# Column DFT by parity of rows in the second layer, sums of halves that accumulate, and another opening

## The chip, the cores and the metric

One core of one Trainium2 chip runs the whole kernel. The metric is the device time of one execution in microseconds (us). Five engines work side by side: TensorE (PE, matrix products; its weight loads are PEld), VectorE (DVE), ScalarE (ACT), GpSimd (POOL) and SyncE (SP), which issues transfers; DMA queues move data between HBM and the on-chip memory. PSUM is the memory of eight banks into which TensorE writes.

## The reference

Two layers, each an FNet step (Fourier mixing of a sequence of 2048 rows and 640 hidden columns) and a gated linear unit of width 1728:

```python
def _A_ref(x, dft_seq_re, dft_seq_im, dft_hid_re, dft_hid_im):
    a = jnp.einsum("bsd,ed->bse", x, dft_hid_re)
    b = jnp.einsum("bsd,ed->bse", x, dft_hid_im)
    return jnp.einsum("ts,bse->bte", dft_seq_re, a) - jnp.einsum("ts,bse->bte", dft_seq_im, b)

def _B_ref(x, w_gate, w_up, w_down):
    g = jnp.einsum("bsd,df->bsf", x, w_gate)
    u = jnp.einsum("bsd,df->bsf", x, w_up)
    return jnp.einsum("bsf,fd->bsd", _sigmoid(g) * u, w_down)

x = A_x
x = x + _A_ref(_layernorm(x), ...)      # layer 1
x = x + _B_ref(_layernorm(x), ...)
x = x + _A_ref(_layernorm(x), ...)      # layer 2
x = x + _B_ref(_layernorm(x), ...)
```

## The kernel before

All values are float32, and each product is made of f16 parts: a number is split into a high and a low part, and hi x hi, hi x lo and lo x hi are added in PSUM. The four DFT matrices have the symmetries of cosine and sine; the kernel uses them to fold x by columns and by rows, so that the products are of a quarter of the size. x stays on the chip, as 16 row tiles of 128.

**One FNet step.** `fold_columns` (L627, L628, DVE) adds and subtracts column d and column 640 - d; `fold_rows` (L667 to L673) and `fold_join` (L707 sums on DVE, L709 high parts on ACT, L715 low parts on DVE) do the same for row s and row 2048 - s. The reversed rows that this takes come from TensorE: `turn_round` (L355) multiplies by a reversed identity into the pair of banks `twin`, and `turned` (L361, ACT) takes them out. Layer norm is folded in: `stats` of each row (L420 on DVE, or ACT), `smeans` and `power` (L377, L403, L404 on GpSimd), `scale` (L408 to L413, L656 on DVE). The opening does this for four groups of rows, 0 to 3, taken from HBM; layer 2 does it block by block, as the layer before ends.

Then `sequence(i, tp)` (L846, L850, TensorE, 18 matmuls of 256 columns) multiplies by the matrix along the sequence: group i, even or odd (EV, OD) outputs. `evict_sums` (L241 on ACT, L243 on DVE) takes the sums out as high and low parts, z. `hidden(q, ph)` (L923, TensorE) multiplies half ph of z by the hidden matrix, for row block q: 9 matmuls for its real part and 8 for its imaginary part, of 321 columns. There are four row blocks and two halves, so eight such products in a layer, and `hidden_middle` (9 matmuls with one row). `evict_hidden` (L959 on ACT, L964 on DVE), `combine` (L989), `join_hidden` (L996) and `add_hidden` (L1009) on DVE form the four outputs that the symmetries give, and add them to x. For q = 0 this is on the way to the next layer norm; the other row blocks follow later, beside products.

**One gated unit.** `norm_*` (L443 on DVE, L430 and L431 on ACT, L453, L463, L465) normalizes a row tile, `transpose_pe` (L569) turns it on TensorE, `gate_up` (L1134) makes the gates and `seven` (L1181, L1274, L1269) the products of later blocks with fewer multiplications, `down` (L1338) the second matrix, whose sums L1353 (DVE) adds to x. Four blocks of rows; these take most of TensorE's time.

**What sets the order.** Everything is placed by hand. The string `OPENING` lists the jobs of the opening and of layer 1's DFT in the order in which they are issued: "seq 3 0" is `sequence(3, EV)`, "hid 0 0" `hidden(0, 0)`, "jlo 3 e" the low part of the even fold of group 3, "evhi 0 1 2" and "ev 0 1 2" the eviction of sums. After it TensorE's work stands in the list `steps`, and `at(u, f, ...)` puts a job of the other engines beside step u. Each engine runs its own queue in order. `Slots` gives out the on-chip memory. The matrix parts for the hidden products (`load_wh`, `split_wh`, keys "h") are split in layer 1 and kept in HBM for layer 2.

Of the kernel before, what the change touches and what calls it, by code (L numbers as in the profile page):

```python
# [16 lines left out]
P = 128  # L17
# [13 lines left out]
EC = EH + 1  # L31
EPS = 1e-5
# [39 lines left out]
FIX = XU + 2 * XTU + WDU  # L72


class Slots:

    LOOK = {4: 2, 5: 6}

    def __init__(self, big):
        self.big = big
        self.live = {}
        self.freed = {}
        self.clock = 0
        self.close = False

    def take(self, n, high):
        taken = sorted(self.live.values())
        if self.close:  # L90

            ends = [FIX] + [d for _, d in taken]
            free = [(a, b) for a, b in zip(ends, [c for c, _ in taken] + [UNITS]) if a + n <= b]
            assert free, f"no room for {n}: {taken}"
            if high:
                a = [a for a in range(UNITS - n, FIX - 1, -n) if all(a + n <= c or d <= a for c, d in taken)][:high]
                if a:
                    return self.new(min(a, key=lambda a: max(self.freed.get(u, 0) for u in range(a, a + n))), n)
                a = max(b for _, b in free) - n
            else:  # L100
                a = min((a for f in free for a in {f[0], f[1] - n}),
                        key=lambda a: (max(self.freed.get(u, 0) for u in range(a, a + n)), a))
            return self.new(a, n)
        found = []
        for i in range(UNITS):
            a = UNITS - (i + 1) * n if high else FIX + i * n
            if a < FIX or a + n > UNITS:
                break
            if all(a + n <= c or d <= a for c, d in taken):
                found.append(a)  # L110
                if len(found) == self.LOOK.get(n, 3):
                    break
        if not found:
            found = [a for a in range(FIX, UNITS - n + 1) if all(a + n <= c or d <= a for c, d in taken)][:1]
        assert found, f"no room for {n}: {taken}"
        age = lambda a: max(self.freed.get(u, 0) for u in range(a, a + n))
        return self.new(min(found, key=age), n)

    def new(self, a, n):
        s = Slot(self.big[:, a * UNIT : (a + n) * UNIT], (a, a + n))  # L120
        self.live[id(s)] = s.span
        return s

    def give(self, s):
        self.clock += 1
        del self.live[id(s)]
        for u in range(*s.span):
            self.freed[u] = self.clock


class Slot:
    def __init__(self, ap, span):
        self.f32, self.span = ap, span
# [19 lines left out]
    turn 0 B, turned 0 B, turn 0 C, turned 0 C, turn 1 B, chi 0 0, means 0, chi 1 0, square 0 C, stats 0 A,  # L153
    col 0 0, stats 0 D, turned 1 B, turn 1 C, col 0 1, clo 0 0, square 0 B, turned 1 C, clo 1 0, double 0 0,
    smeans 0, double 0 1, stats 1 A, means 1, stats 1 D, col 1 0, col 1 1, chi 1 1, square 1 B, clo 1 1,
    square 1 C, power 0, turn 2 B, double 1 1, turned 2 B, turn 2 C, scale 0, stats 2 A, ro 0 0, chi 1 2, chi 0 1,
# [19 lines left out]
    wslo 3 0, wslo 4 0, wslo 4 1"""  # L176

ON_ACT = {(2, GA), (2, GD), (3, GA), (3, GD)}
NORM_ACT, APPLY_ACT, COPY_ACT = {0, 3}, {3}, {3}


@with_exitstack
# [1733 lines left out]
```

## Time and profile before

| | |
|---|---|
| median of 3 runs | 1143.39 us (1142.93 to 1144.43) |
| span of the profiled execution | 1142.6 us |
| TensorE busy | 1107.9 us |
| VectorE busy | 757.1 us |
| ScalarE busy | 521.8 us |
| GpSimd busy | 372.3 us |
| TensorE's idle time before the first long run of matmuls of 512 columns at 109.68 us | some 28 us |

Read it by stage: the opening (to about 66.7 us) folds x while TensorE waits; then TensorE works through layer 1's hidden products and the gated units without pauses; at 603.7 us the head of layer 2 begins (folds of the last row block, sequence and hidden products, the norm of the first rows), and its gated units run from 634 us to the end. Matmuls are pipelined, so the time of one is taken from an unbroken piece of the chain of waits divided by its count, not from the mean of a group.

### The profile page before, as it was taken

The numbers are of one execution on the slowest core, as the hardware profiler recorded it, in microseconds if no ns is written. First come the engines' busy times: TensorE is split into PE (matmuls) and PEld (weight loads), VectorE is DVE, ScalarE is ACT, GpSimd is POOL, SyncE is SP. The second block draws the span as 40 slices with busy tenths as digits, with TensorE's granted clock in tenths as the row PEclk, the third lists the DMA queues.
The fourth block names the chain that finished last, engine by engine and source line by source line (L and its number), as shares of the span: only waits on it lengthen the run. The fifth ranks groups of instructions, "written<-read, shape, count | busy, mean of one in ns | idle before, by whom it ended". The sixth has DMA issues, their size and how long they took to land.

```text
span 1142.6 us, 23152 instructions
## 1 busy us (share of the span) xinstructions
PE 1107.9 (97%) x8918; PEld 876.1 (77%) x8918; DVE 757.1 (66%) x1686; ACT 521.8 (46%) x1129; POOL 372.3 (33%) x584
## 2 busy tenths in 40 slices
PE   5599999999999999999999999999999999999997
PEld 2377446788878887888877888778887888788875
DVE  7995888867756777576657767815773568526740
ACT  5975475254524653265524445314551455225420
POOL 2313574432545454422430136021453113221000
PEclk9999999999999999999999999999999999999999
DMA  8427587858495868867412377575658853896401
GB/s 256 145 67 258 199 310 210 256 189 265 153 261 179 263 205 163 276 227 263 155 70 93 106 224 213 133 240 182 210 150 234 285 179 124 159 250 205 149 18 38
DMA packets 156434, 215.94 MB, mean 189 GB/s; under 512 B 74720, under 2 KB 101493, under 8 KB 156314
## 3 DMA queue, kind: packets, MB, share of 16 engines
q1 hardware_dynamic: 137754, 166.44, 48.1%
q0 software_dynamic: 18560, 47.93, 13.8%
q8 instruction: 72, 1.18, 0.4%
q14 instruction: 48, 0.39, 0.1%
HBM read 173.45 MB, written 26.26 MB: 175 GB/s over the span
## 4 chain that ended last, share of the span: by engine, by line
PE 89%; DVE 5%; DMA 2%; ACT 2%; issue 1%; POOL 1%; SPq 0%; DVEq 0%; POOLq 0%; ACTq 0%
PE acc L1181 42%; PE acc L1338 31%; PE acc L1134 10%; PE acc L1274 2%; PE acc L923 2%; PE acc L846 1%; DMA big<-in_ct 1%; DVE big L243 1%; PE twin L355 1%; DMA big<-kept_w 0%; DMA big<-in_wd 0%; DVE big L715 0%; DVE big L673 0%; DVE big L1009 0%; DVE big L707 0%
## 5 line engine op out<-in xcount | busy, mean ns | idle before, releaser
L1181 PE MATMUL acc<-big 128*128 128x256 f16 x4698 | 516.4, 273 | 0.2 <-ACT big L1185 0.2
L1181 PEld LDWEIGHTS <-big 128*128 128x128 f16 x4698 | 459.7, 98 | 54.6 <-issue 0.3
L1338 PE MATMUL acc<-big 128*128 128x320 f16 x2624 | 357.7, 299 | 0.0
L1338 PEld LDWEIGHTS <-big 128*128 128x128 f16 x2624 | 256.8, 98 | 99.5
L1387 POOL DMA_DIRECT2D big<-in_ct x256 | 174.8, 688 | 217.0 <-DVE big L1396 132.8
L1185 ACT ACTIVATE big<-acc 128x256 f32<-128x256 f32 x348 | 128.6, 380 | 237.0 <-PE acc L1181 235.6
L1371 ACT ACTIVATE big<-big 128x768 f32<-128x768 f32 (+8 forms) x104 | 79.6, 765 | 118.4 <-DVE big L1396 83.4
L1249 DVE TENSOR_TENSOR big<-big 128x512 f16<-128x512 f32 x87 | 59.9, 688 | 100.3 <-ACT big L1248 100.0
L1134 PE MATMUL acc<-big 128*128 128x256 f16 (+1 forms) x705 | 114.8, 325 | 1.1 <-DVE big L243 1.1
L1134 PEld LDWEIGHTS <-big 128*128 128x128 f16 x705 | 68.6, 98 | 46.2 <-DVE big L243 1.6
L1353 DVE SCALAR_TENSOR_TENSOR big<-acc,big 128x320 f32<-128x320 f32 x64 | 28.4, 484 | 99.4 <-PE acc L1338 99.3
L1227 ACT ACTIVATE big<-big 128x512 f32<-128x512 f32 x87 | 53.5, 627 | 45.2 <-DVE big L1218 44.6
L243 DVE SCALAR_TENSOR_TENSOR big<-big 128x640 f16<-128x640 f32 (+5 forms) x80 | 64.3, 839 | 9.9 <-ACT big L241 6.8
L241 ACT ACTIVATE big<-big 128x640 f16<-128x640 f32 (+6 forms) x80 | 50.2, 667 | 36.3 <-DMA big<-big 11.0
L1237 DVE SCALAR_TENSOR_TENSOR big<-acc,big 128x256 f32<-128x256 f32 x87 | 36.3, 418 | 40.5 <-PE acc L1181 34.4
L1404 POOL DMA_DIRECT2D big<-in_ct x40 | 27.3, 685 | 109.7 <-ACT big L1185 65.3
L1218 DVE TENSOR_TENSOR big<-big,acc 128x512 f32<-128x512 f32 x87 | 59.1, 679 | 3.6 <-PE acc L1181 3.4
L1248 ACT ACTIVATE big<-big 128x512 f16<-128x512 f32 x87 | 54.5, 626 | 9.6 <-DVE big L1239 8.8
L1217 DVE TENSOR_TENSOR big<-big 128x256 f32<-128x256 f32 x87 | 36.3, 417 | 15.6 <-ACT big L1185 15.5
L521 ACT ACTIVATE big<-big 128x384 f16<-128x384 f32 (+2 forms) x48 | 28.8, 648 | 29.3 <-DVE big L503 15.7
L1394 DVE TENSOR_TENSOR big<-big 128x256 f32<-128x256 f32 x64 | 26.8, 419 | 21.3 <-DMA big<-in_ct 21.2
L923 PE MATMUL acc<-big 128*128 128x321 f16 (+2 forms) x290 | 40.9, 300 | 0.0
(206 smaller groups left out, 1040.9 us busy)
## 6 DMA issues: line engine op xcount, KB each, us to landing
big<-kept_s SPq DMA_DIRECT2D x84, 512.0 KB
big<-kept_w SPq DMA_DIRECT2D x115, 320.0 KB
big<-in_ct POOLq DMA_DIRECT2D x256, 128.0 KB, 4.1
big<-kept_w SPq DMA_DIRECT2D x74, 192.0 KB
kept_w<-big SPq DMA_DIRECT2D x27, 320.0 KB
big<-in_ct POOLq DMA_DIRECT2D x32, 256.0 KB, 5.0
kept_s<-big SPq DMA_DIRECT2D x13, 512.0 KB
big<-in_wg SPq DMA_DIRECT2D x18, 320.0 KB
```

Of the source, the lines that this page charges most:

```text
L243: nc.vector.scalar_tensor_tensor(dl, src, s, dh, op0=OP.mult, op1=OP.subtract)
L923: nc.tensor.matmul(ps[:m, :EC], z[:, at : at + m], w[:, 384 * wp : 384 * wp + EC], start=(d == 0 and zp == HI and wp == HI), stop=(d == ND ...
L1134: nc.tensor.matmul(ps, w[wp][:, d * P : (d + 1) * P], xt[:, xp, :], start=(d == 0 and wp == HI and xp == HI), stop=(d == ND - 1 and wp == LO))
L1181: nc.tensor.matmul(ps, wt, xt, start=start and n == 0, stop=n == len(todo) - 1, skip_group_check=not start)
L1185: nc.scalar.activation(dst, ps, AF.Copy)
L1218: nc.vector.tensor_tensor(v, v, other, op=OP.add)
L1227: nc.scalar.activation(v, v, AF.Sigmoid, scale=SG)
L1248: nc.scalar.activation(s.parts[HI], v, AF.Copy)
L1249: nc.vector.tensor_tensor(s.parts[LO], v, s.parts[HI], op=OP.subtract)
L1338: nc.tensor.matmul(held["pd", e][0][:, :EH], held["ht", j].parts[hp][:, i * P : (i + 1) * P], held["w", 2, j].parts[wp][:, e * EH : (e + 1 ...
L1371: nc.scalar.activation(v, v, AF.Square, accum_out=new_sum()[:p])
L1387: nc.gpsimd.dma_start(v[:, g], bass.AP(ct.tensor, (r * S + row) * S, [[P, NS], [d * S, 16], [1, P]]))
```

## The change

1. In layer 2 the hidden products use one more symmetry: hidden index d and 320 - d. Rows of the hidden matrix are loaded by parity (`load_wh` with a stride of two rows, `fold_columns` writes even and odd columns apart), and only 161 of the 321 output columns are multiplied, for even and for odd rows into halves E and O of a bank. `unfold` makes the 321 columns again as E + O and E - O. Layer 1 stays at 321 columns (`wide`). For it the matrix is read from HBM and split a second time, instead of being kept.
2. Where halves ph = 0 and 1 of a row block were taken out of PSUM one by one and added by DVE, the second accumulates in PSUM onto the first, after ACT has copied the first: in layer 1 for all row blocks, in layer 2 for q = 0. The difference is then 2u - v.
3. In the opening the means, the edge copies and the first row's sum go from GpSimd to ScalarE, the variances to VectorE, and the power -0.5 to ScalarE's `Abs_reciprocal_sqrt` with one step of refinement on VectorE (`root`, `root_step`). `twin` becomes two pairs of banks, with four banks of sums in place of six until the turning is done.
4. `OPENING` is in another order, and so is the head of layer 2; the last `down` product of layer 1 is split by column halves, with the folds of its rows in halves. The sums and additions of row blocks 2 and 3 come earlier in the first block.
5. `Slots` takes its places from a planner that knows all uses beforehand (`find_homes`).

The core of the diff:

```diff
-    jhi 3 o, ev 0 0 1, join 3 e, jhi 3 e, jlo 3 o, seq 2 0, wshi 1 0, jlo 3 e, hid 0 0, wslo 1 0, seq 3 0, difhi 0,
+    seq 2 1, jhi 3 o, join 3 e, wshi 1 1, jhi 3 e, wshi 1 0, jlo 3 o, seq 2 0, jlo 3 e, ev 0 0 2, ev 0 0 1, whlo 2,
+    seq 3 0, evhi 1 0 2, evhi 1 0 1, evhi 1 0 0, wslo 1 1, hid 0 0, seq 3 1, first 0, ev 1 0 2, ev 1 0 0, ev 1 0 1,
...
+    twins = [twin_pool.tile([P, 2, 512], F32, name=f"twin{k}") for k in range(2)]
...
     def turned_means(i):
-        nc.gpsimd.tensor_scalar(t[:, GB:GD, 12], t[:, GB:GD, 20], 1.0 / D, None, op0=OP.mult)
+        nc.scalar.activation(t[:, GB:GD, 12], t[:, GB:GD, 20], AF.Copy, scale=1.0 / D)
...
+    def root(t, to):
+        nc.scalar.activation(t[:, :, 15], t[:, :, 14], AF.Abs_reciprocal_sqrt, scale=1.0 / to**2)
...
-    def product(ps, ph, r, at, m):
-        for d, n in enumerate(KT[r]):
+    def product(ps, ph, r, at, m, more=False):
+        even, odd, both = (slice(0, EC),) * 3 if wide else (slice(0, EW), slice(EW, EQ), slice(0, EQ))
+        for d, c in ((1, both), (0, even), (2, odd)):
+            n = KT[r][d]
...
-                    nc.tensor.matmul(ps[:m, :EC], z[:, at : at + m], w[:, 384 * wp : 384 * wp + EC],
-                                     start=(d == 0 and zp == HI and wp == HI), stop=(d == ND // 2 and zp == LO))
+                    nc.tensor.matmul(ps[:m, c], z[:, at : at + m], w[:, 384 * wp : 384 * wp + c.stop - c.start],
+                                     start=(not more and d == 1 and zp == HI and wp == HI),
+                                     stop=(d == ND // 2 and zp == LO), skip_group_check=more)
...
+    def unfold(s, v, on=nc.vector):
+        on.tensor_tensor(s[:, :, :EW], v[:, :, :EW], v[:, :, EW:], op=OP.add)
+        on.tensor_tensor(s[:, ::-1, EH : EW - 1 : -1], v[:, :, : EW - 1], v[:, :, EW : EQ - 1], op=OP.subtract)
...
-            order = [(hidden, 0, 0), (hidden, 1, 0), (sequence, 2, EV), (sequence, 2, OD), (sequence, 3, EV),
-                     (sequence, 3, OD), (hidden, 0, 1), (hidden, 2, 0), (hidden, 3, 0), (hidden, 1, 1), (hidden, 2, 1),
-                     (hidden, 3, 1), (hidden_middle,)]
+            order = [(hidden, 1, 0), (sequence, 0, OD), (sequence, 1, OD), (sequence, 2, EV), (sequence, 3, EV),
+                     (hidden, 0, 0), (hidden, 0, 1), (sequence, 2, OD), (sequence, 3, OD), (hidden, 1, 1), (hidden, 2, 0),
+                     (hidden, 3, 0), (hidden_middle,), (hidden, 2, 1)]
...
-            run(he + 12, [(transpose_pe, 0), (transpose_pe, 1)])
+            run(he + 12, [(evict_hidden, 3, 0), (transpose_pe, 0), (transpose_pe, 1), odd[5][1]])
```

TensorE's queue in layer 2 before, at the joint of the real part of hid 0 0 (into bank 67) and its imaginary part (bank 64):

```order
8838 L923 LDWEIGHTS big
8839 L923 MATMUL acc_67<-big 128x321
8840 L923 LDWEIGHTS big
8841 L923 MATMUL acc_64<-big 128x321
8842 L923 LDWEIGHTS big
8843 L923 MATMUL acc_64<-big 128x321
```

The same queue after, inside the real part of hid 1 0, which now comes first; L1031 is the line that was L923:

```order
8761 L1031 LDWEIGHTS big
8762 L1031 MATMUL acc_64<-big 128x322
8763 L1031 LDWEIGHTS big
8764 L1031 MATMUL acc_64<-big 128x161
8765 L1031 LDWEIGHTS big
8766 L1031 MATMUL acc_64<-big 128x161
```

Three matmuls of a part stay at 322 columns (both halves E and O), the rest have 161; their number and their weight loads stay.

VectorE's queue in the head of layer 2 before, from the last evictions of sums (L243) to the first row's statistics; 964 takes hid 0 1 out of PSUM, 996 joins the halves, 1009 adds to x:

```order
884 L243 SCALAR_TENSOR_TENSOR big<-acc_66,big 128x512
885 L243 SCALAR_TENSOR_TENSOR big<-acc_67,big 128x512
886 L243 SCALAR_TENSOR_TENSOR big<-acc_64,big 128x512
887 L964 SCALAR_TENSOR_TENSOR big<-acc_69,big 128x321 x2
888 L996 TENSOR_TENSOR big<-big 128x642
889 L1009 TENSOR_TENSOR big<-big 128x2x321
890 L1009 TENSOR_TENSOR big<-big 128x2x319
891 L443 BN_STATS small_81<-big 128x6 x2
```

The same place after; 267 evicts sums, 1099 takes the accumulated product, 1072 and 1073 unfold, 1181 adds to x:

```order
889 L267 SCALAR_TENSOR_TENSOR big<-acc_366,big 128x512
890 L267 SCALAR_TENSOR_TENSOR big<-acc_66,big 128x512
891 L267 SCALAR_TENSOR_TENSOR big<-acc_67,big 128x512
892 L1099 SCALAR_TENSOR_TENSOR big<-acc_64,big 128x322 x2
893 L1072 TENSOR_TENSOR big<-big 128x2x161
894 L1073 TENSOR_TENSOR big<-big 128x2x160
895 L1181 TENSOR_TENSOR big<-big 128x2x321
896 L1181 TENSOR_TENSOR big<-big 128x2x319
897 L488 BN_STATS small_79<-big 128x6 x2
898 L489 BN_AGGR small_79<-small_79 128x2
```

The join of halves has gone from this place and two unfolding operations have come in; the odd sums, which were all evicted ahead of it, are in part evicted after it.

VectorE's queue at the last fold of the opening before: 145 is "jlo 3 e", the low part of group 3's even fold, and 141 an eviction of sums:

```order
140 L673 SCALAR_TENSOR_TENSOR big<-big,quad_79 128x321
141 L243 SCALAR_TENSOR_TENSOR big<-acc_68,big 128x512
142 L707 TENSOR_TENSOR big<-big 128x321 x2
143 L715 TENSOR_TENSOR big<-big 128x2x320
144 L718 COPY big<-big 128x4x64
145 L715 TENSOR_TENSOR big<-big 128x2x321
146 L243 SCALAR_TENSOR_TENSOR big<-big 128x640 x2
```

After, the same fold stands at 148, and two evictions of sums follow it directly:

```order
143 L769 SCALAR_TENSOR_TENSOR big<-big,quad_77 128x321
144 L267 SCALAR_TENSOR_TENSOR big<-acc_363,big 128x512
145 L806 TENSOR_TENSOR big<-big 128x321 x2
146 L814 TENSOR_TENSOR big<-big 128x2x320
147 L817 COPY big<-big 128x4x64
148 L814 TENSOR_TENSOR big<-big 128x2x321
149 L267 SCALAR_TENSOR_TENSOR big<-acc_364,big 128x512
150 L267 SCALAR_TENSOR_TENSOR big<-acc_67,big 128x512
```

Before that fold VectorE evicts sums six times in the order before, four times after.

More of the change, by code (lines that the diff above doesn't have):

```diff
@@ L72, with __init__ @@
 FIX = XU + 2 * XTU + WDU
+NEAR = (60, 25, 8, 1)
 class Slots:
[L79 to L84, printed above, removed]
+    def __init__(self, big, homes=None):
+        self.big, self.homes = big, homes
+        self.asked = []
         self.clock = 0
-        self.close = False
     def take(self, n, high):
[L89 to L117, printed above, removed]
@@ L152 @@
 OPENING = """
[L153 to L156, printed above, removed]
-    smeans 1, turned 2 C, whhi 1, col 2 0, double 1 0, power 1, re 0 0, clo 1 2, ro 0 1, scale 1, whhi 2, ro 1 1,
```

502 lines of the change are left out of this document (346 added, 156 removed).

## The prediction

> **What bounds the kernel now.** I read the page's busy times and slices first, then the windows by stage, the timelines of TensorE (PE) and VectorE (DVE) where a window shows idle time, and last the chain of waits.
>
> ```profile
> span 1142.6 us, 23152 instructions
> PE 1107.9 (97%) x8918; PEld 876.1 (77%) x8918; DVE 757.1 (66%) x1686; ACT 521.8 (46%) x1129; POOL 372.3 (33%) x584
> PE   5599999999999999999999999999999999999997
> ```
>
> TensorE is busy for 1107.9 of 1142.6 us; 34.7 us are idle, by the slices almost all in the first two and at the very end. Elsewhere only fewer matmul columns save time. Five windows show the two stages that the change touches (columns after the length: PE, PEld, DVE, ACT, POOL busy, then the clock):
>
> ```profile
> 20.00:40.00 20.00, 7.55 (x14) 3.73 (x14) 17.20 (x48) 17.55 (x40) 8.21 (x10) 1.00 0.88 292
> 40.00:57.00 17.00, 11.67 (x75) 8.72 (x74) 16.31 (x41) 15.29 (x33) 4.22 (x14) 0.90 0.13 42
> 57.00:66.63 9.63, 9.19 (x75) 6.95 (x72) 9.56 (x20) 6.94 (x15) 0.21 (x1) 0.99 0.38 98
> 66.69:108.60 41.91, 41.84 (x367) 33.89 (x367) 28.56 (x54) 25.77 (x48) 12.66 (x16) 1.00 0.50 162
> 603.70:634.20 30.50, 29.80 (x240) 21.95 (x238) 25.28 (x57) 16.44 (x34) 3.44 (x6) 1.00 0.28 98
> ```
>
> Up to 66.63 VectorE sets the pace (9.56 of the last 9.63 us): it folds x for the DFT, and the last fold releases the last sequence products. From there TensorE is full (41.84 of 41.91). The head of layer 2, in the last row, has TensorE busy for 29.80 of 30.50 us, but VectorE is at 25.28 there too, so both are near their limits.
>
> The joints of the opening, from the timelines (start, length, what, and the idle time before it in brackets):
>
> ```profile
> 7.50 2.50 PE L355 MATMUL twin<-big 128*128 128x320 f32 x4 [0.88 <-ACT big L361]
> 7.48 0.83 DVE L627 TENSOR_TENSOR big<-big 128x640 f32<-128x640 f32 x1 [1.48 <-ACT big L361]
> 10.87 0.82 DVE L627 TENSOR_TENSOR big<-big 128x640 f32<-128x640 f32 x1 [0.79 <-ACT big L361]
> 20.82 0.17 DVE L408 TENSOR_TENSOR quad<-quad 128x4 f32<-128x4 f32 x1 [0.53 <-POOL quad L404]
> 25.55 0.70 DVE L243 SCALAR_TENSOR_TENSOR big<-big 128x514 f16<-128x514 f32 x1 [1.65 <-ACT big L241]
> 26.46 0.17 DVE L408 TENSOR_TENSOR quad<-quad 128x4 f32<-128x4 f32 x1 [0.22 <-POOL quad L404]
> 66.69 3.89 PE L846 MATMUL acc<-big 128*128 128x256 f16 x34 [0.50 <-DVE big L715]
> 109.68 10.53 PE L1134 MATMUL acc<-big 128*128 128x512 f16 x48 [1.14 <-DVE big L243]
> ```
>
> **The narrower products of layer 2.** Prices of a matmul come from unbroken pieces of the chain (start, length, what, how many):
>
> ```profile
> 70.58 13.96 PE acc L923 x102
> 559.34 44.43 PE acc L1338 x327
> 640.88 1.24 PE acc L569 x20
> 1011.47 71.39 PE acc L1181 x654
> L569 PEld LDWEIGHTS <-big 128*128 128x128 f16 x80 | 4.9, 98 | 1.3 <-DVE big L465 0.9
> ```
>
> So 321 columns take 13.96/102 = 0.1369 us, 320 columns 0.1359, 256 columns 0.1092: 0.417 ns per column more. Down that line 161 columns take 0.0697 us, 322 columns 0.1367. The transposes, 128 columns, take 0.062 where the line gives 0.056, so the line may be 6 ns too low: 0.076 at most that way. The loads of weights last 98 ns each, but twenty followed one another in 1.24 us there, so they overlap one another.
>
> Before, a product of layer 2 is 9 + 8 = 17 matmuls of 321 columns, 2.327 us. After, it is 3 of 322 and 6 of 161, then 3 of 322 and 5 of 161: 6 x 0.1367 + 11 x 0.0697 = 1.587 us. That is 0.740 less, 5.92 for eight. The middle row's 9 matmuls lose 957 columns, 0.40 us. Together **-6.3 us**, with 0.076 instead -5.7 (94 matmuls of 161 x 6 ns back). If each narrow matmul instead waited for its own 98 ns load, 94 x 28 ns = 2.7 us would come back and -3.6 remain. I take -6.3, since the transposes are the nearest row.
>
> The Trainium skill, "TensorE: Matmul & The Clock Gate", section "Back-to-back issue gap", speaks against this: it gives about 81 ns per matmul for a stream of weight load and matmul at 128 columns. By that a 161-column matmul would cost at least 81 ns, and the saving would be 5.2 us as an estimate. The transposes, at 62 ns a matmul in such a stream, are below that figure here.
>
> **What VectorE pays for it.** The outputs now come as even and odd halves, and each row block needs two more operations to unfold them, of 322 and 320 elements:
>
> ```profile
> L707 DVE TENSOR_TENSOR big<-big 128x321 f32<-128x321 f32 x2 | 0.9, 486 | 0.0
> 634.00:662.00 28.00, 28.00 (x237) 22.11 (x236) 20.98 (x35) 11.04 (x18) 2.50 (x9) 1.00 0.51 138
> ```
>
> Sixteen at 0.486 are 7.8 us. Four lie in the head, the others in stretches where VectorE has 7 of 28 us free, under TensorE's products; those cost nothing. The column folds now read every second element. A split that also reads so took 0.69 us for 516 elements, and 0.69 for 512 read straight:
>
> ```profile
> 50.68 0.69 DVE L243 SCALAR_TENSOR_TENSOR big<-big 128x516 f16<-128x516 f32 x1
> 52.39 0.68 DVE L243 SCALAR_TENSOR_TENSOR big<-acc,big 128x512 f16<-128x512 f32 x1
> ```
>
> So striding is free.
>
> **The head of layer 2.** Two chains must stay hidden. Their pieces before:
>
> ```profile
> 603.79 0.89 DVE big L1353 x2
> 613.56 3.56 PE acc L846 x31
> 619.48 0.45 ACT big L959
> 624.20 0.93 ACT big L431 x2
> 625.74 0.73 POOL small L404
> 631.57 0.83 DVE big L465
> ```
>
> The first, from the last sums of the layer before to the folds, takes 613.56 - 603.79 = 9.8 us. The change splits the last down product and folds its half columns early, so some 2 us of it go ahead of TensorE's last matmul, and 1.6 of odd folds behind the even ones; what is left, about 7 us, has hid(1,0) and two sequence products in front of it (1.6 us and 36 x 0.1092 = 3.9 us, beside the last half of the down product). The second chain, from the last product of block 0 to the turned rows, runs from 619.48 to 632.40, 12.9 us, with five more products (85 x 0.1369 = 11.6 us) and the first transposes beside it. After, the rows' sums come from accumulated halves, one row's statistics go to ScalarE, and I get about 9.5 to 10.4 us: eviction 0.45, two sums 0.9, unfolding 0.9, adding 1.6, statistics 1.1, the root's chain 1.8, centring and two parts 2.4, up to 1.3 for evictions in between. Beside it stand only two sequence products and three narrow hidden ones: 3.9 + 4.8 = 8.7 us. A stall of 0.8 to 1.7 us, against 0.64 now:
>
> ```profile
> 613.56 3.56 PE L846 MATMUL acc<-big 128*128 128x256 f16 x31 [0.29 <-DVE big L715]
> 631.55 0.73 PE L569 MATMUL acc<-ident,big 128*128 128x128 f16 x10 [0.19 <-DVE big L465]
> 632.45 0.45 PE L569 MATMUL acc<-ident,big 128*128 128x128 f16 x5 [0.16 <-DVE big L465]
> ```
>
> I take **+0.6**, bounds -0.3 and +2.
>
> **The opening.** Per group, GpSimd's means, squares and power go away:
>
> ```profile
> 34.48 2.88 POOL L377 TENSOR_SCALAR quad<-quad 128x4 f32<-128x4 f32 x1 [6.70 <-ACT big L369]
> 37.45 1.82 POOL L403 TENSOR_SCALAR quad<-quad 128x4 f32<-128x4 f32 x1
> 39.35 1.03 POOL L404 TENSOR_TENSOR quad<-quad,half 128x4 f32<-128x4 f32 x1
> ```
>
> These waits cost VectorE little (0.53, 0.22 above), as it is kept fed by other groups. All its idle time from 7.48 us to the last fold comes to 3.7 us (0.79, 1.65 and 0.53 are the largest). Its work before that fold hardly changes: two evictions of sums fewer (-1.2), one group's statistics moved in from the idle time before 7.48 (+1.1). So the last fold can't end before 66.6 - 3.7 = 62.9 us. ScalarE, at 17.55 of 20 us there, takes over the means, an edge copy, the root and one load of its tables more:
>
> ```profile
> L361 ACT ACT_TABLE_LOAD x1 | 1.3, 1283 | 0.7 <-PEq L1909 0.7
> ```
>
> I let about half of the idle time stay as new waits behind ScalarE and the data: 64.6 us, bounds 62.9 and 67.
>
> What follows that fold on TensorE grows. Before, two hidden products fill its waits ahead of 66.69; after, hid 0 0 stands behind seq 3 0, and with it all eight stand behind the last fold: 34 x 0.1369 = 4.65 us more. The gap of 1.14 at 109.68 goes, as the weights' low parts are now split ahead of the gated sums. New stalls at the turned rows (only hid 2 1 and the middle row cover them) I put at 0.9, bounds 0.3 and 2.5. Together: (64.6 - 66.6) + 4.65 - 1.14 + 0.9 = **+2.4 us**, bounds +0.1 and +6.4.
>
> The Trainium skill, "ScalarE: Activation LUTs", section "What ACT_TABLE_LOAD costs", adds a drain of about 1380 ns to each load. By that the opening would lose up to 1.4 us more, as an estimate; the row above shows the load alone and no drain.
>
> **Sum.** -6.3 + 0.6 + 2.4 = -3.3 us. The profiled span of 1142.6 us becomes 1139.3; it stands 0.8 below the median of 1143.39, which becomes 1140.1. 0.2% of it, what a measurement of this kernel can tell from no change, is 2.3 us.
>
> **The rivals.**
> - *The opening keeps its length.* VectorE closes its gaps, the fold ends at 62.9 and the stalls are small: -6.3 + 0.6 + 0.1 = -5.6, 1137.8 us. For it: POOL's 5.7 us chain is gone, and a second pair of banks frees the turning from one wait of about 0.9 us each. Against: the rows show 3.7 us at most to win. Chance 0.20.
> - *The norm chain of layer 2's head decides, and it is slower.* With the products short, 8.7 us lie beside the chain that takes 12.9 now. If it keeps that length, TensorE stands 4.2 us there instead of 0.6, so the saving falls from 6.3 to 2.7; with the opening's loss at 5 us (fold at 66, stalls 2.1) the sum is +2.3 to +3, some 1146 us. It decides from a chain of about 12 us with the opening that late. For it: VectorE is at 25.28 of 30.50 us, and three more evictions come into that stretch (2 us). Chance 0.20.
> - *The weight load sets the narrow matmul.* At 98 ns the saving is 3.6: -3.6 + 0.6 + 2.4 = -0.6, no change, 1142.8 us. Against: the transposes at 62 ns. Chance 0.12.
>
> **How the numbers follow.** The forecast has 0.48; its bounds, not all on one side at once, give 1137 to 1143. The range takes in the first rival and most of the second: 1136 to 1146. Faster by over 0.2%: 0.38 of the forecast's 0.48 and the first rival's 0.20, 0.58. Within: 0.08, the third's 0.11 and 0.04 of the second, 0.23. Slower: the rest, 0.19.
>
> **What would show it.** In the profile after: narrow hidden products of 161 columns at 70 ns (98 would be the third rival) and a head of layer 2 with under 2 us of idle TensorE (over 4 is the second). In the opening, the last fold's end (62.9, 64.6 or 67 us) and the first long run of 512 columns, now at 109.68, at about 112. I am wrong if the opening ends before 109 or after 116, or if TensorE gets idle time in the blocks, which the change should leave alone.

## The result, and the profile after

The changed kernel takes **1152.07 us** (1150.30 to 1156.05, 4 runs) against 1143.49 us (now 4 runs): a ratio of 1.0081 (95% interval 1.0061 to 1.0101), 8.6 us slower. A run's time stands 1.8 us above its span in both kernels. The profiled execution of the changed kernel is the shortest of its four (1148.5 us of span), that of the kernel before the longest of its four (1142.6 us). So the traces hold 5.9 us of difference; what the other executions of the changed kernel lose beyond that was not profiled. In one later kernel (c1) the profiled execution ran throughout at a granted clock of 0.75; its comparison rests on its other runs, and it was profiled again as c1_again.

The page after: TensorE is busy for 2.4 us less, and the span is longer. The clock, all nines before, now begins with 7 and 8.

```profile
span 1148.5 us, 23222 instructions
PE 1105.5 (96%) x8918; PEld 875.6 (76%) x8918; DVE 764.7 (67%) x1729; ACT 537.5 (47%) x1179; POOL 345.3 (30%) x547
PE   4599999999999999999999999999999999999997
PEclk7788999999999999999999999999999999999999
```

The span falls into three pieces at two marks that both kernels have: the start of layer 2's hidden products on TensorE, and the start of the products of seven (L1181 before, L1356 after). After, from the timeline and the chain of waits:

```profile
608.09 1.76 PE L1031 MATMUL acc<-big 128*128 128x322 f16 x17
663.72 16.38 PE acc L1356 x150
```

and before:

```profile
603.73 4.82 PE L923 MATMUL acc<-big 128*128 128x321 f16 x34
661.70 18.34 PE acc L1181 x168
```

Two sequence products (36 x 0.1092 = 3.93 us) moved from the first piece into the second. With that taken out:

| piece | before | after | difference |
|---|---|---|---|
| to layer 2's start | 603.73 | 608.09, with 3.93 us less to do | +8.3 |
| head of layer 2 | 57.97 | 55.63, with 3.93 us more to do | -6.3 |
| products of seven to the end | 480.9 | 484.8 | +3.9 |

**The head did what was forecast; the opening lost 8.3 us where 2.4 were forecast, and 3.9 us were lost in a stretch that the forecast called untouched.**

The opening, from TensorE's timeline after (start, length, what, idle time before it). L946 are sequence products, L1031 hidden products, L653 the transposes of the normalized rows ("turned rows" below), L1309 the gates that need them:

```profile
65.95 1.93 PE L946 MATMUL acc<-big 128*128 128x256 f16 x16 [0.57 <-DVE big L814]
72.00 13.23 PE L1031 MATMUL acc<-big 128*128 128x321 f16 x94
87.07 0.45 PE L653 MATMUL acc<-ident,big 128*128 128x128 f16 x5 [1.84 <-ACT big L528]
88.07 1.78 PE L653 MATMUL acc<-ident,big 128*128 128x128 f16 x15 [0.54 <-DVE big L531]
90.11 0.37 PE L1309 MATMUL acc<-big 128*128 128x256 f16 x1 [0.26 <-ACT big L661]
90.83 5.07 PE L1309 MATMUL acc<-big 128*128 128x256 f16 x29 [0.35 <-DVE big L663]
```

Before, the first gates (L1134) run without such a wait:

```profile
87.17 3.45 PE L1134 MATMUL acc<-big 128*128 128x256 f16 x30
```

The last fold releases TensorE at 65.95 (66.69 before): -0.7. Two hidden products more stand behind it: +4.65. The gap at 109.68 is gone: -1.1. TensorE waits 3.0 us at the turned rows (1.84 + 0.54 + 0.26 + 0.35). And after those waits it is slow: 29 matmuls take 5.07 us where 29 x 0.1092 is 3.17, 15 transposes 1.78 where 15 x 0.062 is 0.93: +2.75. Together +8.5, against +8.3 in the table. The windows show the granted clock there (PE busy first, the clock third from the end):

```profile
85.00:88.00 3.00, 0.69 (x7) 0.28 (x5) 2.17 (x6) 3.00 (x6) 0.00 (x0) 0.94 0.54 215
88.00:91.00 3.00, 2.32 (x18) 1.83 (x18) 1.21 (x7) 1.84 (x4) 0.73 (x1) 0.50 0.00 0
```

TensorE works 0.69 of 3 us, and then its clock is at 0.50. (The 7, 7 and 8 of the first three slices stand for an earlier fall: from 12 to 66 us the clock is 0.68 on average, 0.97 before. VectorE sets the pace there, and what that fall costs was not separated.) ScalarE's queue shows a part of what TensorE waited for: the statistics of row 3 (L476, L477) stand ahead of the high parts of rows 0 and 1 (L528), whose scale VectorE had ready at 84.5 us (L421). That holds the high parts back by about 1.0 us.

```profile
83.81 0.72 ACT L476 ACTIVATE big<-big 128x640 f32<-128x640 f32 x1
84.34 0.17 DVE L421 SCALAR_TENSOR_TENSOR small<-small 128x2 f32<-128x2 f32 x1
84.66 0.83 ACT L477 ACTIVATE big<-big,small 128x640 f32<-128x640 f32 x1
85.49 1.53 ACT L528 ACTIVATE big<-big,small 128x640 f16<-128x640 f32 x2
```

The third piece: four waits of TensorE for ScalarE, 3.3 us together, none of which the kernel before has. The two largest, and the wait of VectorE that stands behind the first of them:

```profile
896.98 65.66 PE L1356 MATMUL acc<-big 128*128 128x256 f16 x600 [1.56 <-ACT big L1360]
1090.33 2.45 PE L1356 MATMUL acc<-big 128*128 128x256 f16 x21 [1.14 <-ACT big L1360]
866.38 1.14 DVE L587 TENSOR_SCALAR big<-big,small 128x640 f32<-128x640 f32 x2 [8.98 <-DMA big<-big]
DVE big L587 <- DMA big<-big: 27.5, 3, 10.6
```

The same two places of TensorE in the kernel before:

```profile
886.84 71.56 PE L1181 MATMUL acc<-big 128*128 128x256 f16 x654
1084.42 2.45 PE L1181 MATMUL acc<-big 128*128 128x256 f16 x21
```

VectorE writes the normalized rows of the next block into a tile named "pf" and stands 8.98 us for a transfer that still reads there. The planner had put pf(2, 1), the one of block 2, on the place of pb(2, 0), the source of a transposing transfer, one step after that tile was given back (a step is one taking or giving back of a tile). Behind it on VectorE wait the sums of the down product and the tests of the inputs (L1571), behind these a store that GpSimd issues, behind the store the loads of further tests (L1562), and behind a test ScalarE's queue (L1546), which frees TensorE's banks (L1360):

```profile
876.03 1.08 POOL L427 DMA_INDIRECT out<-big,rows  x1 [16.68 <-DVE big L1571]
894.68 0.43 DVE L1569 TENSOR_TENSOR big<-big 128x256 f32<-128x256 f32 x1 [1.36 <-DMA big<-in_ct]
895.72 0.84 ACT L1546 ACTIVATE big<-big 128x768 f32<-128x768 f32 x1 [4.47 <-DVE big L1571]
```

### The profile page after: what moved, and what is told of

The parts are those of the page before. It is cut to its first block, busy times and chain, and to the rows that moved or that the text cites. A ratio compares the mean times of both kernels' runs of the same rounds, so it can differ in the third digit from the quotient of the medians.

```text
span 1148.5 us, 23222 instructions
## 1 busy us (share of the span) xinstructions
PE 1105.5 (96%) x8918; PEld 875.6 (76%) x8918; DVE 764.7 (67%) x1729; ACT 537.5 (47%) x1179; POOL 345.3 (30%) x547
## 5 line engine op out<-in xcount | busy, mean ns | idle before, releaser
L1356 PE MATMUL acc<-big 128*128 128x256 f16 x4698 | 516.7, 273 | 3.3 <-ACT big L1360 3.3
L1356 PEld LDWEIGHTS <-big 128*128 128x128 f16 x4698 | 459.6, 98 | 58.1 <-issue 4.1
L1513 PEld LDWEIGHTS <-big 128*128 128x128 f16 x2624 | 256.7, 98 | 99.5
L1562 POOL DMA_DIRECT2D big<-in_ct x256 | 174.5, 687 | 261.7 <-DVE big L1571 171.0
L1360 ACT ACTIVATE big<-acc 128x256 f32<-128x256 f32 x348 | 128.0, 381 | 209.8 <-PE acc L1356 198.4
L1546 ACT ACTIVATE big<-big 128x768 f32<-128x768 f32 (+10 forms) x110 | 81.6, 742 | 117.7 <-DVE big L1571 83.9
L1309 PE MATMUL acc<-big 128*128 128x256 f16 (+1 forms) x705 | 116.6, 328 | 0.6 <-DVE big L663 0.3
L1309 PEld LDWEIGHTS <-big 128*128 128x128 f16 x705 | 69.8, 99 | 46.2 <-issue 1.0
L267 DVE SCALAR_TENSOR_TENSOR big<-big 128x640 f16<-128x640 f32 (+6 forms) x82 | 60.9, 777 | 11.2 <-ACT big L265 8.9
L265 ACT ACTIVATE big<-big 128x640 f16<-128x640 f32 (+7 forms) x82 | 51.0, 658 | 22.7 <-POOL big L1247 7.3
L946 PE MATMUL acc<-big 128*128 128x256 f16 (+2 forms) x288 | 39.7, 299 | 14.0 <-ACT big L808 9.0
L946 PEld LDWEIGHTS <-big 128*128 128x128 f16 x288 | 29.8, 106 | 23.1 <-ACT big L808 10.5
L1568 DVE TENSOR_TENSOR big<-big 128x256 f32<-128x256 f32 x64 | 26.7, 417 | 26.2 <-DMA big<-in_ct 25.8
```

The lines of the kernel that those rows point to most:

```text
L267: nc.vector.scalar_tensor_tensor(dl, src, s, dh, op0=OP.mult, op1=OP.subtract)
L946: nc.tensor.matmul(o, xv[:, 384 * xp + P * d : 384 * xp + P * (d + 1)], moving(r, cps[cp]), start=(i % 2 == 0 and r == 0 and xp == HI and ...
L1309: nc.tensor.matmul(ps, w[wp][:, d * P : (d + 1) * P], xt[:, xp, :], start=(d == 0 and wp == HI and xp == HI), stop=(d == ND - 1 and wp == LO))
L1356: nc.tensor.matmul(ps, wt, xt, start=start and n == 0, stop=n == len(todo) - 1, skip_group_check=not start)
L1360: nc.scalar.activation(dst, ps, AF.Copy)
L1513: nc.tensor.matmul(held["pd", e][0][:, :EH], held["ht", j].parts[hp][:, i * P : (i + 1) * P], held["w", 2, j].parts[wp][:, e * EH : (e + 1 ...
```

## The experiments

**Places, cover, columns and clock.** "Cover" is work that TensorE has while it would otherwise wait. The first edit, in the planner:

```diff
 def find_homes(asked):
+    asked = [(n, t0, t1 + 12 * (n == NT)) for n, t0, t1 in asked]
```

> The changed kernel with one line more in the planner of on-chip places: a tile that a transposing transfer reads ('pb') counts as in use for 12 steps longer, so that the next tile of unturned rows ('pf') is not put on top of it. Theory (places): in the changed kernel VectorE stands 8.98 us at L587 in block 2 of layer 2, since pf was put on the pb that a transfer still read; everything behind it on VectorE, the stores that GpSimd issues and the test loads come late, and TensorE stands 1.56 and 1.14 us. Then these two waits go (TensorE's idle time after 663 us falls from 3.3 to under 1 us), the span comes out near 1145.5 us, and the runs, which were spread over 1150.3 to 1156.1, draw together. Rival (VectorE's work): the unfolding and the earlier joins make VectorE late by themselves; then the waits stay and the span stays at 1148.5 us or above.

1146.62 us (ratio 1.0027, 1.0016 to 1.0038). VectorE's wait at L587 is gone, while e_hid3, e_fill and e_cols below, which leave the planner alone, have 27 to 32 us of it. Of TensorE's waits in the blocks 0.26 and 1.14 us are left:

```profile
710.03 2.45 PE L1357 MATMUL acc<-big 128*128 128x256 f16 x21 [0.26 <-ACT big L1361]
1084.39 2.45 PE L1357 MATMUL acc<-big 128*128 128x256 f16 x21 [1.14 <-ACT big L1361]
```

The theory of places holds, in part: from the products of seven to the end it takes 482.5 us instead of 484.8. The span of 1142.5 us is lower than expected because the opening was 3.7 us shorter too in this execution: the last fold came 1.06 us earlier (64.89) and the clock stayed up behind the waits (the gates' 30 matmuls in 3.61 us). The ten runs fall into two groups, 1143.9 to 1145.5 and 1147.8 to 1148.2: what that gap is was not profiled, but its some 3 us are near what the fall of the clock costs (below, at e_cols).

```diff
-    nst 2, mid, hid 2 1, nst 3, nhi 0, nhi 1, nlo 0, nlo 1, cen 2,
+    nst 2, mid, hid 2 1, hid 3 0, nst 3, nhi 0, nhi 1, nlo 0, nlo 1, hidev 2 1, hidev 3 0, hid 3 1, cen 2,
```

> The changed kernel with hid 3 0 and hid 3 1 moved from behind the first gate product to ahead of the turned rows (4.65 us of matmuls), and the copies of block 2 and 3 with them. Theory (cover): TensorE's waits of 3.0 us at 87 to 91 us (1.84, 0.54, 0.26, 0.35) and the slow clock that follows them (29 matmuls of the gates in 5.07 us where 3.2 is the pace) come from the missing cover; they go, and layer 2 begins at about 603.3 us instead of 608.09. Rival (chain): ScalarE's chain is simply longer and the copies of the hidden products, now ahead of it, push it back further; then the wait stays above 1.5 us and layer 2 begins after 606.

1146.53 us (1.0034, 1.0020 to 1.0048); layer 2 begins at 604.65 us. Between the two: the clock stays, the first 29 gate matmuls take 3.33 us, but waits of 1.8 us in four pieces come in instead (two for ScalarE, one of them for the copy of a hidden product, and two for VectorE). Cover is part of the cause, the order of the other engines' work the rest.

For the next, the line that clears `wide` is left out, and the sums and differences of layer 2 are formed without unfolding:

```diff
-            at(block[2], wide.clear)
```

> The changed kernel with layer 2's hidden products left at 321 columns (the flag wide is never cleared, no unfolding), everything else as changed. Theory (columns): the narrow products are worth what was worked out for them, 6.3 us: from the start of layer 2's hidden products to the start of the products of seven takes 55.6 us in the changed kernel and would take about 61.5 here. Rival (chain): the head is bound by the chain of norms, and wide products fit into its cover: the stretch grows by under 3 us. If VectorE's unfolding were what delays the blocks, TensorE's idle time after 663 us (3.3 us) would fall here; by the theory of places it stays about the same.

1158.07 us (1.0124, 1.0090 to 1.0157). The head, from TensorE's timeline and the chain:

```profile
607.89 2.49 PE L1031 MATMUL acc<-big 128*128 128x321 f16 x17
668.66 11.35 PE acc L1360 x104
```

60.77 us against 55.63: the narrow products bring **5.1 us** here (5.7 with the waits left out, 0.23 us against 0.83). Counted from start to start, the 145 matmuls themselves take 19.95 us here and 13.79 in the changed kernel, 6.2 us less; the rest is the wait of 0.60 us at the transposes and the start behind it. Waits in the blocks grew instead of falling (2.40 and 2.82 us the largest), so they do not need the unfolding; but the plan of places is another one here too.

The filler is two more products of the middle row into a spare bank, between hid 2 1 and the first turned rows:

```diff
-wld 4 0, tp 1, tp 0,
+wld 4 0, fill, tp 1, tp 0,
```

> The changed kernel with 18 matmuls of 321 columns more (2.5 us, their sums are not used) on TensorE ahead of the first turned rows, where it stands 1.84 us; no other work is moved. Theory (clock): the idle time there makes the granted clock fall to 0.5 to 0.6 for some 8 us; with the filler the clock stays at 1, the gates' first 29 matmuls take 3.2 instead of 5.07 us and the transposes 0.9 instead of 1.78, so layer 2 begins 2 to 3 us earlier (about 605.5) although nothing useful was added. Rival: the slow matmuls have another cause (waits for banks or weights within the run); then layer 2 begins at 608 or up to 0.6 us later.

1149.75 us (1.0059, 1.0042 to 1.0076). With 2.5 us of work added for nothing:

```profile
72.89 15.78 PE L1032 MATMUL acc<-big 128*128 128x321 f16 x112
88.60 1.36 PE L654 MATMUL acc<-ident,big 128*128 128x128 f16 x20
90.66 3.61 PE L1320 MATMUL acc<-big 128*128 128x256 f16 x30 [0.70 <-ACT big L662]
```

The gates run at pace, and layer 2 begins at 606.76 us although its last fold came 0.9 us later than in the changed kernel (66.83): counted from the fold, 2.2 us earlier. That agrees with the theory of the clock, but it does not show that the filler kept the clock up, for the next kernel has no filler and its clock stayed up too.

**The tests.** Left out: the operation that tests the symmetry of the narrow products, which the change added.

```diff
-        nc.vector.scalar_tensor_tensor(b, a[:, : EW - 1], turns()[: b.shape[0]], a[:, EH : EW - 1 : -1], ...)
-        square_sum(b)
+        turns()
```

> The changed kernel without the one operation (and its square) that the test of the hidden matrix got for the narrow products, six times in block 3 of layer 2; that symmetry is then not tested. Theory (tests): TensorE's wait of 1.14 us near the end of the products of seven (at 1090.33 us in the changed kernel, and 1.14 us in every kernel so far) comes from this: ScalarE waits for VectorE's test operations and takes the sums out of the banks late. Then that one wait goes and the others (0.34, and up to 1.6 us in block 2) stay. Rival (unfolding or places): the wait stays.

1153.76 us, one run. The place near the end has no wait any more:

```profile
1091.94 1.80 PE L1449 MATMUL acc<-big 128*128 128x256 f16 x15
1093.73 2.45 PE L1356 MATMUL acc<-big 128*128 128x256 f16 x21
```

That wait is the test's. The others differ from execution to execution (here 2.43 us in block 2, and 2.30 for a transfer).

This kernel also settles what the fall of the clock costs, for its opening is that of the changed kernel. TensorE waits as long at the turned rows (1.84, 0.55 and 0.69 us) and works 0.68 of the 3 us around the first of these waits, but the clock stays at 1.00:

```profile
86.76 0.45 PE L653 MATMUL acc<-ident,big 128*128 128x128 f16 x5 [1.84 <-ACT big L528]
89.46 3.61 PE L1309 MATMUL acc<-big 128*128 128x256 f16 x30 [0.69 <-ACT big L661]
```

From the last fold to the long run of gates (at 98.93 us here, 101.51 in the changed kernel) it takes 33.29 us against 35.56. **So the fall costs 2.3 us, and the same waits can go with it or without it.** e_homes and p8 (below) repeat the pair: their longest waits there are 1.48 and 1.49 us, and the stretch takes 32.93 us with the clock up and 35.46 with the fall.

**Four repairs at once, and what went wrong.** Row block 3's sums were moved back with the rest:

```diff
-    at(... block[0] + (9.6 if q == 2 else 15.6) + n, f, q, *a)
+    at(... (block[0] + 9.6 if q == 2 else block[1] + 3.5) + n, f, q, *a)
```

> The changed kernel with four repairs: the planner's hold of transposed tiles; hid 3 0 and hid 3 1 ahead of the turned rows, with row 3's statistics behind the high parts of rows 0 and 1 on ScalarE; the six column tests of the hidden matrix 1.2 steps apart instead of 0.9; the sums and additions of row block 3 back at the start of block 1. By the theory of places and cover the waits after 663 us go (2 to 3 us), those at the turned rows fall under 1 us and the clock stays: a span near 1140 us, 2 to 3 us below the kernel before. If the opening's loss lies in the products behind the last fold alone, the span ends near 1142 to 1143.

> As the kernel with four repairs, but hid 3 0 and hid 3 1 stay where the change put them; only row 3's statistics go behind the high parts of rows 0 and 1 on ScalarE (1.65 us of ScalarE ahead of them now). Theory (order on ScalarE): the first wait at the turned rows, 1.84 us, falls to about 0.3 and the clock stays at 1; within 1 us of the kernel with four repairs. If it is the missing cover instead, TensorE still waits over 1.5 us there, and the clock falls in some runs.

1163.55 us (1.0175, 1.0158 to 1.0192) and 1168.81 us (1.0219, 1.0202 to 1.0236): both far off. The later sums hold their tiles longer; the planner then finds no plan for a distance of 60, 25 or 8 steps and takes one for 1, in which tiles are reused one step after they are given back, and TensorE waits all over (b1, waits by line):

```profile
PE acc L1514 <- DVE big L1501: 3.0, 1, 3.0
PE acc L1357 <- DMA big<-kept_w: 2.9, 1, 2.9
PE acc L1310 <- ACT big L266: 2.8, 1, 2.8
```

So the same was done without that move, and with the planner asked for a distance of 10 and a hold of 8 steps:

> The changed kernel with the planner alone changed: transposed tiles held 8 steps longer, and a distance of 10 steps between two uses of a place asked for first (the kernels with four repairs, at 1163 and 1168 us, had been placed with a distance of 1, the changed kernel with 8). Theory (places): the time hangs on the places; with this plan no waits of over 0.5 us but the 1.14 us of the tests are left after 130 us, and the median is 1145 to 1147 us, with layer 2's start still set by the opening. Rival: the 20 us of the two repaired kernels came from their other edits; then this plan gives no more than the hold of 12 steps did, or less.

> As p8, with hid 3 0 and hid 3 1 ahead of the turned rows, row 3's statistics behind the high parts, and the six column tests 1.2 steps apart. Theory (places): without the move of row block 3's sums the plan stays good, and the 20 us of the first attempt are gone; waits at the turned rows under 2 us together, none of 1.14 us near the end: a median of 1142 to 1144 us. Rival (these edits are themselves bad): over 1150 us again.

> As c1, but hid 3 0 and hid 3 1 stay behind the first gate product. Theory (cover): TensorE waits 1 to 2 us more than in c1 at the turned rows, and the clock falls there in some of the runs (3 us): a median of 1144 to 1147 us with a wide spread. Theory (order on ScalarE): the same as c1 within 1 us.

p8: 1145.78 us (1.0024, 1.0014 to 1.0034). c1: **1143.75 us** (1.0001, 0.9992 to 1.0010). c2: 1145.82 us (1.0022, 1.0013 to 1.0032). No move of row block 3, no 20 us. Two things differ between b1 and c1, the move and the planner's setting. The planner, run by itself, tells which decides: for b1 without the move it finds a plan for 8 steps, for c1 with the move only one for 1.

p8 changes nothing but the places, and its median is 6.3 us below the changed kernel's. That is more than the 2.1 us that its profile gains from the products of seven to the end (482.7 us against 484.8): the profiled execution of p8 is the longest of its ten, with a wait of 1.47 us in layer 1, and that of the changed kernel its shortest. The other 4 us no trace explains. In c2, row 3's statistics moved without the cover, the first wait falls from 1.84 to 0.62 us, but 2.37 us appear ahead of the gates, where ScalarE now copies out the turned rows too late: that order alone only moves the wait.

c1 takes all of the loss back, and its second profile tells where:

> The same kernel as c1, whose profiled execution fell to a granted clock of 0.75 and shows nothing. Theory (places and cover): no wait over 0.6 us after 130 us, two or three waits of under 1.5 us together at the turned rows, layer 2 begins at about 604.5 us with two sequence products fewer ahead of it than before, and the span is 1142 to 1143 us. If instead waits in the blocks are left over, their lines tell which places or tests they hang on.

```profile
604.52 1.76 PE L1032 MATMUL acc<-big 128*128 128x322 f16 x17
91.71 5.10 PE L1310 MATMUL acc<-big 128*128 128x256 f16 x30 [2.12 <-ACT big L662]
```

1144.07 us (1.0009, 0.9999 to 1.0018). From the products of seven to the end it takes 481.2 us, as before the change (480.9): the blocks are mended, some 2 us by the places (p8) and 1.5 us with the tests set further apart. In the opening one wait of 2.12 us is left, with the clock's fall behind it, 5.10 us for 30 matmuls.

**What stands ahead of the last fold.** In the kernel before, hid 0 0 behind seq 3 0:

```diff
-jlo 3 e, hid 0 0, wslo 1 0, seq 3 0, difhi 0,
+jlo 3 e, wslo 1 0, seq 3 0, hid 0 0, difhi 0,
```

> The kernel before with one edit: hid 0 0 moved from ahead of seq 3 0 to behind it, as in the changed kernel's order. Theory: before the last fold TensorE has time to spare and behind it none, so the whole product (17 matmuls, 2.33 us) is added: layer 2 begins at 606.0 instead of 603.73 us and the median rises by 2.2 us. Rival: the product held up the last sequence product or its banks as much, and moving it costs under 1 us.

1147.97 us (1.0044, 1.0028 to 1.0061); layer 2 begins at 606.58 us:

```profile
65.35 1.93 PE L846 MATMUL acc<-big 128*128 128x256 f16 x16 [0.57 <-DVE big L715]
72.42 0.43 PE L923 MATMUL acc<-big 128*128 128x321 f16 x2 [0.85 <-DVE big L964]
606.58 4.82 PE L923 MATMUL acc<-big 128*128 128x321 f16 x34
```

+2.85 us in the profile. TensorE goes on from the last fold 1.34 us earlier than in the kernel before (65.35 against 66.69), so that 4.2 us came in behind it: the product (2.33), new waits of 1.4 us (the largest 0.85), and 0.5 us that are not assigned. The runs rose by more, 4.5 us, which the one profile doesn't explain. The other way round:

> As c1, with VectorE's work before the last fold cut: the low parts of two weight tiles (0.8 us each) go behind it, and hid 0 0 behind seq 3 1, so that TensorE has two sequence products while VectorE catches up. Theory (VectorE sets the opening's end): the last fold ends 1.5 us earlier and layer 2 begins 1 to 1.5 us earlier than in c1. Rival: what VectorE owes is only paid later; TensorE then waits ahead of hid 0 0 and layer 2 begins at the same time as in c1 or later.

> As c1, with hid 3 0 ahead of the last fold again, as in the kernel before: it is put in front of seq 2 1, with one weight tile's low part (0.8 us of VectorE) moved ahead of it, and the two halves of block 3 in layer 1 are taken out one by one again instead of accumulating. Theory (products behind the last fold): 2.33 us of TensorE leave the full stretch and the fold comes 0.8 us later: layer 2 begins 1.5 us earlier than in c1, near 603, and the median is about 1142. Rival: TensorE is not idle there, or the waits at the turned rows grow by what is taken away (they lose 2.3 us of cover): no change against c1.

> As c4, with hid 0 0 ahead of the last fold too: the two evictions of sums that it needs (1.3 us of VectorE) come ahead of that fold. Theory (products behind the last fold): another 2.33 - 1.3 = 1.0 us, layer 2 begins near 602 us, a median of about 1141 us, 2 us below the kernel before. Rival: VectorE bounds the fold, and each operation moved ahead of it costs as much as the product gives; then c5 equals c4.

All three are misses: 1152.66 us (1.0082, 1.0068 to 1.0096), 1147.23 us (1.0043, 1.0027 to 1.0058) and 1149.38 us (1.0056, 1.0043 to 1.0070). In c3 the last fold came no earlier (TensorE goes on at 65.69 us), and a wait of 5.19 us came in block 1 of layer 1. In c4, hid 3 0 stopped TensorE's queue until VectorE had its operands, and seq 2 1, 2 0 and 3 0 stood behind it:

```profile
61.68 2.84 PE L1032 MATMUL acc<-big 65*128 65x321 f16 x10 [7.34 <-DVE big L268]
64.32 6.87 PE L947 MATMUL acc<-big 128*128 128x256 f16 x54
```

They show that the idle time ahead of the fold cannot simply be filled in this order of VectorE's work; that both products back there would give 4.65 us remains argued, by v_late1 for one of them.

**ScalarE's order.** The last wait of c1, mended by the order of ScalarE's work (with `nscale 1`, three short operations of VectorE, behind it):

```diff
-nhi 0, nhi 1, hidev 3 0, hidev 2 1, nlo 0, nlo 1, nst 3, hid 3 1, cen 2, cen 3, nvar 1, npow 1, wld ...
+nhi 0, nhi 1, cen 2, hidev 3 0, hidev 2 1, nlo 0, nlo 1, nst 3, hid 3 1, nvar 1, wld ...
-tpl 0, tpl 1, nscale 1, tph 1, tph 0,
+tpl 0, tpl 1, tph 1, tph 0, npow 1, cen 3, nscale 1,
```

> As c1, with ScalarE's order at the turned rows mended: the centring of row 2 goes into a gap ahead of the copies of hidden products, and that of row 3, with the root, behind the two copies of the turned rows out of PSUM, which now come 2 us of ScalarE later than TensorE needs them. Theory (order on ScalarE, and the clock behind it): the wait of 2.12 us ahead of the gates falls to 0.7, their first 30 matmuls take 3.3 instead of 5.1 us, layer 2 begins 2 to 3 us earlier (about 602), and the median is 1141 to 1142 us, below the kernel before. Rival: rows 2 and 3 are turned as much later, and the wait moves behind the gates: no change against c1.

> As c7, with another plan of the same quality (distance 9 asked for, more turns of the search). Theory (places): within 1 us of c7, since no wait hangs on a place in either. If it is over 1.5 us off, places still set the time in this kernel, though no rule of the plan says which.

c7: **1141.34 us** (0.9985, 0.9976 to 0.9994); c8: 1141.42 us (0.9984, 0.9975 to 0.9993): 2 us faster than the kernel before, and the fastest of all. In c7:

```profile
88.54 1.28 PE L654 MATMUL acc<-ident,big 128*128 128x128 f16 x20
90.41 3.72 PE L1310 MATMUL acc<-big 128*128 128x256 f16 x30 [0.59 <-ACT big L662]
602.84 1.76 PE L1032 MATMUL acc<-big 128*128 128x322 f16 x17
```

The wait falls from 2.12 to 0.59 us, the matmuls run at pace, and layer 2 begins 1.7 us earlier. The two plans of c7 and c8 differ by 0.1 us in the median, although c8's profile has a wait of 1.23 us in the blocks where c7 has 0.26.

## Why the prediction was wrong

The sum was -6.3 + 0.6 + 2.4 = -3.3 us; the trace has -6.3 in head and products together, +8.3, and +3.9. **Two steps failed: the opening's term (+2.4), which sized the stalls at the turned rows too low and had no term for the clock behind them, and "the blocks, which the change should leave alone", which put the new places and the new test at nothing.**

- **The narrow products** were sized right. 17 of them take 1.60 us in an unbroken piece, 1.587 were worked out, so a 161-column matmul goes at 0.070 us, and the 98 ns of a weight load did not hold it up. Nor did the 81 ns that the Trainium skill gives for 128 columns ("TensorE: Matmul & The Clock Gate", "Back-to-back issue gap").

```profile
637.76 1.60 PE acc L1031 x17
```

- **The chains of the head** held too: 0.83 us of waits (0.60 and 0.23) against 0.64 before, where 1.24 was allowed. The rival that saw the head bound by its norm chain did not come. Two slips in the working did no harm: the items of the norm chain add up to 9.2 to 10.5 us, not 9.5 to 10.4, and of the first chain's 9.8 us 6.2 are left, not 7.
- **The last fold** was put at 64.6 us, 2.0 earlier; TensorE went on at 65.95 us, 0.74 earlier: 1.3 us mis-sized, inside the bounds. The kernels with the same order ahead of it have 64.09 to 66.83 us. No run shows how much of this the statistics off GpSimd brought: v_late1, which leaves them there and moves one product, has 65.35. ScalarE's new load of tables cost its 1.28 us and no more, with 0.02 us on either side. The drain of 1380 ns that the Trainium skill adds ("ScalarE: Activation LUTs", "What ACT_TABLE_LOAD costs") is not seen here:

```profile
19.25 0.18 ACT L400 ACTIVATION_READ_ACCUMULATOR big<-big,quad 128x1 f32 x1
19.45 1.28 ACT L414 ACT_TABLE_LOAD   x1
20.75 0.21 ACT L414 ACTIVATE quad<-quad 128x4 f32<-128x4 f32 x1
```

- **The stalls at the turned rows**, 0.9 us with an end of 2.5, measured 3.0: 2.1 us mis-sized. They were judged by the cover alone (hid 2 1 and the middle row); the order in ScalarE's queue was not counted, neither row 3's statistics ahead of the high parts (about 1.0 us) nor the work ahead of its copies of the turned rows (a wait of 2.12 us in c1_again, 0.59 in c7).
- **The clock** was not a term at all. The fall behind the stalls cost 2.3 us by the pair of e_cols and the changed kernel, 2.75 by the slow matmuls.
- **The planner** was not priced, nor was the added test. A new plan of places sets which transfers a write waits for, and so moved VectorE by 9 us at one place. The two cost the 3.9 us of the trace. The plan alone (p8) is worth 6.3 us of median, and why that is more than its profile shows stays open. The spread between runs is not explained either: 5.8 us in 4 runs of the changed kernel, 5.7 in 10 of p8, 3.5 and 4.4 in the two times c1's kernel was run, 2.7 in c7.

Against the forecast span of 1139.3 us the trace has 9.2 us more: the fold 1.3, the stalls 2.1, the clock 2.75, places and tests 3.9, and the head -0.6 add up to that within 0.3. Another 2.8 us of the missed median lie outside the two traces, since the shortest execution after and the longest before were profiled. Of the forecast's own signs two came true: the first long run of 512 columns begins at about 118 us, not 112 (the limit was 116; TensorE makes 20 matmuls from 116 to 118 us, 11 from 118 to 120), and TensorE has idle time in the blocks. With the blocks untouched the opening's 8.3 us alone would have given about 1145.4 us, inside the range that ended at 1146.0; no rival held the cause.

## What to carry to other kernels

A change to memory placement is a change of timing: compare, for each tile that a transfer reads, how soon its place is written again, before calling distant stages untouched. Where an engine waits a few microseconds ahead of dense matmuls, count the slow matmuls behind the wait as a possible cost as well, and look through the queue of the engine it waits for, operation by operation: the order of three jobs on ScalarE was worth 2.4 us here (c1 to c7). Mend one thing at a time; four repairs at once were 20 us slower than the kernel before, by the one that had seemed harmless.

## What the runs showed of the hardware

In the changed kernel the granted clock fell to 0.50 although TensorE was idle there for no longer than 1.84 us at a stretch, with 0.69 of 3 us worked. The waits alone do not decide it. In e_cols, with the same waits and 0.68 of 3 us worked, the clock stayed at 1.00. p8 fell and e_homes did not, with 1.03 and 1.05 of 3 us worked. c2 and c5 both wait 2.37 us ahead of the gates, and 30 matmuls then take 5.10 us in c2 and 3.44 in c5:

```profile
95.17 3.44 PE L1312 MATMUL acc<-big 128*128 128x256 f16 x30 [2.37 <-ACT big L662]
```

In the four profiles whose waits there are all 0.7 us or shorter (e_hid3, e_fill, c7, c8) it did not fall. The Trainium skill ("TensorE: Matmul & The Clock Gate", "What's actually happening") speaks of an idle window of some 3.4 us that runs freely. These runs agree only if a window with some work in it counts as idle, and the free running would explain why the same waits go both ways; no run here tests either.
